# Folding the Fourier mixing of an attention and FNet kernel over features and over four classes of tokens

## The chip, the cores and the metric

The kernel runs on one core of a Trainium2 chip. A core has five engines that work side by side, each through its own instructions in order: TensorE (PE, matrix products, with its weight loads as a second row, PEld), VectorE (DVE), ScalarE (ACT), GpSimd (POOL) and SyncE (SP), which here only issues DMAs. They wait for each other by semaphores. The metric is device time in microseconds (us) of one launch.

## The reference

Two kinds of layer take turns, twice each, on `x` of 2048 tokens by 512 features, all in fp32: softmax attention with 32 heads of 16, and a Fourier mixing that keeps the real part.

```python
def _A_ref(x, wqkv, wo):
    B, S, D = x.shape
    H = 32; Dh = D // H
    qkv = (lambda x, *d: x.transpose(*d))((x @ wqkv).reshape(B, S, 3, H, Dh), 2, 0, 3, 1, 4)
    q, k, v = qkv[0], qkv[1], qkv[2]
    scores = jnp.einsum("bhqd,bhkd->bhqk", q, k) * Dh ** -0.5
    o = jnp.einsum("bhqk,bhkd->bhqd", _softmax(scores, axis=-1), v)
    return (lambda x, *d: x.transpose(*d))(o, 0, 2, 1, 3).reshape(B, S, D) @ wo

def _B_ref(x, dft_seq_re, dft_seq_im, dft_hid_re, dft_hid_im):
    a = jnp.einsum("bsd,ed->bse", x, dft_hid_re)
    b = jnp.einsum("bsd,ed->bse", x, dft_hid_im)
    return jnp.einsum("ts,bse->bte", dft_seq_re, a) - jnp.einsum("ts,bse->bte", dft_seq_im, b)

x = x + _A_ref(_layernorm(x), A_wqkv, A_wo)
x = x + _B_ref(_layernorm(x), ...)
x = x + _A_ref(_layernorm(x), A_wqkv, A_wo)
x = x + _B_ref(_layernorm(x), ...)
```

The four DFT matrices (2048x2048 and 512x512, cosine and sine) are inputs, so the kernel may use their symmetries only if it tests them.

## The kernel before

**Precision.** Where fp32 accuracy is wanted, an operand is split into a high part rounded to the fast format fp32r and a low part, the rest (`split`, L93: ACT writes the high part, DVE or POOL subtracts for the low one), and `mm3` (L102) makes three products. Other fp32 products are not split.

**Projection** (`project`, L266): normalises `x`, transposes it on PE (L321), makes q, k and v, and sends q and k through DRAM. The weights are loaded (`load_w`) and split (`split_w`) by quarters; for layer 2 this is done during the first mixing, by `after.open()`, `after.prepare()` and `split_w` calls between its last products (L953 to L964), and early in projection 2.

**Attention** (`attend`, L587): 32 units `u` (a pair of heads, half of the tokens) of 16 steps `kt`, 512 steps in all. A step makes four score products (`scores`, L511) into two of three PSUM tiles called `sc`, ACT takes the exponential of both (L517, 128x1024 each), and two steps later PE multiplies by the values (`pv`, L532). When a unit is done, `gather` copies its sums (L542), `pack` rearranges them by eight small DMAs on SP, and `normalize` divides (L563 to L566). The loads of the next unit (`load_k`, `load_q`, `load_m`) are issued on POOL's queue. From unit 17 on the `wo` tiles of the first half of the tokens are made between steps, and `fold` runs on POOL at units 21 and 23.

**The symmetry test.** In attention 1 only, the class `Symmetry` streams the token DFT matrix `ct` through free buffers, 32 groups of four tiles, one group at every 7 steps. POOL subtracts entries that should mirror each other, DVE takes the largest absolute value (`amax`, L131). At step 244 `finish` (L178) makes the maximum over partitions: DVE's L190, PE's transpose L192 into an `sc` tile, and DVE's L193 and L194 into `sflag`. At the end of each mixing a branch on `sflag` runs `general`, which uses no symmetry.

**Mixing** (`mix_layer`, L717). Tokens `s`, `1024 - s`, `1024 + s` and `2048 - s` share rows of the DFT, so `fold` (L646) adds and subtracts their four normalised tiles, and four classes `k` of half-size products remain: even and odd tokens, real and imaginary. `accumulate` (L753) multiplies the folded tokens by the split DFT, 48 products of 128x512 for a class; `evacuate` splits the result into `Uh` and `Ul`; `hid` (L860) multiplies by the features' DFT, 24 products per output pair; ACT copies one half out (`osb`, L871), DVE and POOL add to two tiles of `x` (L874 to L880), `layernorm` follows if there is a next layer (L86 to L89; the last step of it, L79, is put off to the next call of `ln_flush`), and SP stores. Two tokens that fold on themselves are `edge` products (L790), whose operands are put on three partitions by small DMAs, and a Nyquist row made apart. All matrices are split anew in each mixing (`split_c`, `split_f`, `load_d`).

The order is written out by hand: two chunks of `accumulate` and the edges, then the last unit's normalisation and the eight `wo` tiles of the second half of the tokens with `fold` of groups 2 and 3 (L807 to L827), then the other products of the even tokens, four `hid`, all products of the odd tokens, four `hid`.

## Time and profile before

| | us |
|---|---|
| median of 3 runs | 2620.58 (2619.74 to 2621.46) |
| the profiled execution | 2620.9 |
| its span, first to last instruction | 2619.1 |
| PE busy | 2494.2 (95%) |
| ACT busy | 2043.3 (78%) |
| DVE busy | 1252.7 (48%) |
| POOL busy | 744.3 (28%) |

The span falls into six stages, cut where one kind of work ends in the timeline: projection 1, attention 1, mixing 1, projection 2, attention 2, mixing 2. A busy share over the whole span is a mean of stages that have different limits, so each stage is read from its own windows, and a wait from its place in the timeline. An engine's idle time is told by the instruction that ended it.

### The profile page before, as it was taken

Reading aid. Unit: us, or ns where it says so; the run is one execution under the profiler, and the core shown is the slowest. Engines: PE = TensorE matmul, PEld = TensorE weight load, DVE = VectorE, ACT = ScalarE, POOL = GpSimd, SP = SyncE. Lnnn points to the kernel's source line nnn. Section 1 sums busy time; section 2 is a strip of 40 time slices with the busy share of each in tenths; the row PEclk is TensorE's granted clock in tenths of the full one; section 3 lists DMA queues with packets and bytes.
Section 4 is the critical chain, followed back from the end, with each engine's and each line's share of the span. In section 5 each row is a group of like instructions: output and inputs, shape, how many; then the busy total and the mean of one; then the engine's idle time right before and its main releaser. Section 6 shows DMA issues by size and latency. Waiting matters only on the chain. (4 is left out here: it accounts for less than half of the span.)

```text
span 2619.1 us, 37733 instructions
## 1 busy us (share of the span) xinstructions
PE 2494.2 (95%) x14853; PEld 1098.1 (42%) x14853; DVE 1252.7 (48%) x1555; ACT 2043.3 (78%) x2324; POOL 744.3 (28%) x1091
## 2 busy tenths in 40 slices
PE   7999999997999999986979999999999999999778
PEld 6753333332343333345767533333333433333456
...
GB/s 189 140 155 126 148 149 118 130 107 28 73 74 53 59 54 46 45 51 119 112 132 141 98 62 56 56 47 45 51 60 67 68 65 49 46 46 46 69 117 114
DMA packets 117132, 223.34 MB, mean 85 GB/s; under 512 B 29860, under 2 KB 38324, under 8 KB 110772
## 3 DMA queue, kind: packets, MB, share of 16 engines
...
## 5 line engine op out<-in xcount | busy, mean ns | idle before, releaser
L517 ACT ACTIVATE P<-sc 128x1024 f32<-128x1024 f32 x2048 | 1880.5, 1191 | 89.7 <-PE sc L511 89.7
L532 PE MATMUL po<-P,V 128*17 128x512 f32 x8192 | 1079.3, 599 | 0.4 <-ACT P L517 0.4
L511 PE MATMUL sc<-qs,ks 64*128 64x512 f32 x4096 | 939.4, 445 | 9.1 <-DMA ks<-kd 5.0
L511 PEld LDWEIGHTS sc<-qs,ks 64*128 64x128 f32 x4096 | 484.5, 184 | 876.0 <-ACT P L517 829.1
L563 DVE RECIPROCAL lpk<-lpk 32x512 f32<-32x512 f32 x128 | 427.6, 3340 | 198.4 <-DMA lpk<-oa 196.0
L542 DVE COPY oa<-po 17x512 f32<-17x512 f32 x256 | 175.9, 687 | 656.8 <-PE po L532 650.7
L257 POOL DMA_DIRECT2D ks<-kd x128 | 65.7, 513 | 968.8 <-PE sc L511 946.1
L532 PEld LDWEIGHTS po<-P,V 128*17 128x17 f32 x8192 | 136.3, 95 | 376.4 <-issue 355.0
L98 ACT ACTIVATE qh<-sc 128x512 fp32r<-128x512 f32 x64 | 38.2, 596 | 130.8 <-PE sc L105 125.9
L164 POOL TENSOR_TENSOR xh<-xh,xh 128x512 f32<-128x512 f32 x96 | 121.1, 1290 | 0.7
L89 POOL TENSOR_TENSOR rs<-ve,mhalf 128x1 f32<-128x1 f32 x64 | 44.9, 702 | 251.2 <-DVE ve L88 251.0
L365 POOL TENSOR_TENSOR sq<-qh 128x512 fp32r<-128x512 f32 x64 | 66.8, 1044 | 160.5 <-ACT qh L98 159.3
L104 PE MATMUL sc<-xTl,wh 128*128 128x512 f32 x256 | 101.2, 395 | 0.5 <-DVE xTl L96 0.4
L105 PE MATMUL sc<-xTh,wl 128*128 128x512 f32 x256 | 101.5, 397 | 0.0
L103 PE MATMUL sc<-xTh,wh 128*128 128x512 f32 x256 | 101.5, 396 | 0.0
L131 DVE TENSOR_REDUCE sym<-xh 128x1 f32<-128x512 f32 (+1 forms) x128 | 76.2, 615 | 51.4 <-POOL xh L164 47.6
L566 DVE TENSOR_TENSOR oT<-opk,oT 32x512 fp32r<-32x512 f32 x128 | 89.7, 700 | 4.4
L95 ACT ACTIVATE fh<-xh 128x512 fp32r<-128x512 f32 x32 | 18.9, 623 | 93.0 <-DVE xh L654 91.2
L564 DVE TENSOR_TENSOR opk<-opk,lpk 32x512 f32<-32x512 f32 x128 | 88.6, 692 | 4.5
L99 DVE SCALAR_TENSOR_TENSOR ql<-sc,qh 128x512 fp32r<-128x512 f32 x64 | 43.9, 687 | 94.7 <-ACT qh L98 93.7
L263 POOL DMA_DIRECT2D qs<-md x128 | 67.1, 525 | 29.3 <-DMA ks<-kd 29.3
L250 POOL DMA_DIRECT2D qs<-qd x128 | 64.7, 506 | 5.2 <-issue 5.2
...
## 6 DMA issues: line engine op xcount, KB each, us to landing
ks<-kd POOLq DMA_DIRECT2D x128, 256.0 KB, 5.0
xh<-ct SPq DMA_DIRECT2D x128, 256.0 KB
qs<-qd POOLq DMA_DIRECT2D x128, 128.0 KB, 5.4
ks<-kd POOLq DMA_DIRECT2D x128, 128.0 KB, 4.2
...
```

Source lines behind the costliest of these rows:

```text
L103: nc.tensor.matmul(ps, ah, bh, start=start, stop=False)
L104: nc.tensor.matmul(ps, ah, bl, start=False, stop=False)
L105: nc.tensor.matmul(ps, al, bh, start=False, stop=stop)
L131: nc.vector.reduce_max(self.m[:n, self.col:self.col + 1], d, axis=AX.X, apply_absolute_value=True)
L164: nc.gpsimd.tensor_tensor(T[g], T[g], T[0], op=op)
L511: nc.tensor.matmul(pss[hd][:, qb * 512:qb * 512 + 512], k[r:r + 64, kt * 128:kt * 128 + 128], q[r:r + 64, qb * 512:qb * 512 + 512], start= ...
L517: e = nc.scalar.activation(pt, pss[hd], AF.Exp)
L532: nc.tensor.matmul(o[32 * j:32 * j + DH + 1, :], self.V[:, kt, 2 * p + hd, :], P[hd][:, qb * 512:qb * 512 + 512], start=kt == 0, stop=kt = ...
L542: nc.vector.tensor_copy(oa[32 * j:32 * j + DH + 1, :], o[32 * j:32 * j + DH + 1, :])
L563: nc.vector.reciprocal(lpk[rr, c], lpk[rr, c])
L564: nc.vector.tensor_tensor(opk[rr, c], opk[rr, c], lpk[rr, c], op=ALU.mult)
L566: nc.vector.tensor_tensor(ot[rr, 1, c], opk[rr, c], ot[rr, 0, c].bitcast(F32), op=ALU.subtract)
```

## The change

Features are put into the order 0, 256, 1 to 255, 511 to 257 outside the kernel, and `fold` now also folds feature `j` with `512 - j`: 16 operations of 255 or 257 columns for 8 of 512, and classes of half the width again. Tokens 0 to 255 stand for four outputs each (`t`, `1024 - t`, `1024 + t`, `2048 - t`), so a layer has eight `hid` of 13 products with 256 or 258 columns, and the sums and differences of an even and an odd result (`combine`, `finish`) give the four tiles. Single tokens are rank-one fp32 products (`crow`, `drow`) and four `corners`. `Symmetry` also tests the features' DFT (36 groups, one at every 6.5 steps), and its POOL work writes the split DFT matrices to DRAM (`keep_c`, `halves`), from where mixing loads them. The split weights of projection 1 are written to DRAM (`save_w`) and loaded again (`open_w`). Folded groups 0 and 1 are split by POOL during attention (`split_g`, units 24 and 25; `fold` at units 21 and 22). The mixing begins with the even tokens' products over groups 0 and 1, which are all the data that they need.

```diff
 class Symmetry:
+        self.groups += [("d", part, c) for part in range(2) for c in range(2)]
+        self.m = pool_.tile([128, 200], F32, name="sym")
...
+    def halves(self, src, fixes=()):
+        n, w = src.shape
+        h = self.pool.tile([128, 258], F32R, name="symh", bufs=2)
+        l = self.pool.tile([128, 258], F32R, name="syml")
+        nc.gpsimd.tensor_copy(h[:n, :w], src)
...
+        nc.gpsimd.tensor_tensor(l[:n, :w], src, h[:n, :w].bitcast(F32), op=ALU.subtract)
...
+    def keep_c(self, T, part, i, j):
...
+        for hl, t in enumerate(self.halves(T[0][:, :w], fixes)):
+            c0 = 128 * (j % 2)
+            t = t.bitcast(F32)
+            nc.sync.dma_start(cs[k, half, hl, :, i % 2, c0:c0 + 128], t[:, 0:128])
...
     def mirror(self, d, t, part, i, j):
+        g.tensor_tensor(d[:, 256:384], t[:, 128:256], t[:, 0:128], op=op2)
...
+    def reduce(self):
+        self.mx = self.pool.tile([128, 1], F32, name="symmx")
+        nc.vector.reduce_max(self.mx, self.m, axis=AX.X)
+
     def finish(self):
         ps = sc_tile()
-        nc.tensor.transpose(ps[:1, :128], mx, ident)
+        nc.tensor.transpose(ps[:1, :128], self.mx, ident)
+        lim = self.pool.tile([1, 1], F32, name="symlim")
         nc.vector.reduce_max(sflag, ps[:1, :128], axis=AX.X)
-        nc.vector.tensor_tensor(sflag, sflag, self.scale, op=ALU.is_le)
+        nc.vector.tensor_tensor(lim, self.scale[:, 0:1], self.scale[:, 1:2], op=ALU.min)
+        nc.vector.tensor_scalar(lim, lim, TOL, None, op0=ALU.mult)
+        nc.vector.tensor_tensor(sflag, sflag, lim, op=ALU.is_le)
...
     def attend(self):
-                if i < 8 and i % 4 == 0 or i >= 8 and i % 7 == 1:
-                    sym.load(i // 4 if i < 8 else 1 + i // 7)
-                if i % 7 == 6:
-                    sym.compare(i // 7)
+                for n in range(len(sym.groups)):
+                    if i == max(0, 13 * n // 2 - 12):
+                        sym.load(n)
+                    if i == 13 * n // 2 + 6:
+                        sym.compare(n)
+                if i == 10:
+                    sym.finish_special()
                 if i == 244:
+                    sym.reduce()
+                if i == 262:
                     sym.finish()
...
+            if u == 0 and kt == 1 and self.first:
+                self.save_w()
...
 def fold(i, p_, tag, engine):
+    m = [t1[:, 0:255], t1[:, 255:510], t2[:, 0:255], t2[:, 255:510]]
+    for x, d in zip(X, m):
+        tt(d, x[:, 2:NR], x[:, NR:], ALU.subtract)
+        tt(x[:, 2:NR], x[:, 2:NR], x[:, NR:], ALU.add)
...
 def mix_layer(at, x_src, x_dst, after):
+    def product(out, k, half, ch, c):
+        f = features(k, ch)
+        ch_, cl_ = C[k, half]
+        for i in (2 * half, 2 * half + 1):
+            gh, gl = G[k // 2, i]
+            for n, (g, w) in enumerate(((gh, ch_), (gh, cl_), (gl, ch_))):
+                nc.tensor.matmul(out, g[:, f], w[:, i % 2, c], ...)
+        if (k, half) == (0, 0):
+            nc.tensor.matmul(out, z[0:1, f], crow[0:1, c], start=False, stop=True)
+
+    def seq(half):
+        t1, t2, t3 = sc_tile(), sc_tile(), sc_tile()
...
+    load_c(0, 0)
+    at.pack(2 * NP - 1, *at.last, engine=nc.scalar)
...
+    for k, out, row in seq(0):
+        evacuate(k, out, row, 0)
...
     for t in range(8, 12):
         at.wo_mm(t, wps[t - 8], range(ND - 1))
     for qb in range(2):
         at.normalize(2 * NP - 1, qb, *at.last)
     for t in range(8, NT):
...
         if t == 12:
             ln_flush()
             fold(2, bl, "tf", nc.vector)
+            split_g(2, nc.scalar, nc.gpsimd)
     ln_flush()
     fold(3, bl, "tf", nc.vector)
+    split_g(3, nc.scalar, nc.gpsimd)
     at.ab.release()
+    if after is not None:
+        after.open_w()
...
+    def hid(cls, q):
+        ps = sc_tile()
+        re, im = ps[:, 0:258], ps[:, 512:768]
...
+        nc.scalar.activation(ims[:, 2:NR], im[:, 0:255], AF.Copy)
+        return re, ims
+
+    def combine(engine, re, ims, name, bufs):
+        zt = br.tile([128, 767], F32, name=name, bufs=bufs)
+        engine.tensor_tensor(zt[:, 0:NR], re[:, 0:NR], ims, op=ALU.subtract)
+        engine.tensor_tensor(zt[:, NR:512], re[:, 2:NR], ims[:, 2:NR], op=ALU.add)
+        engine.tensor_tensor(zt[:, 512:767], re[:, 2:NR], ims[:, 2:NR], op=ALU.subtract)
+        return zt
...
+            re, ims = hid(cls, q)
+            res = br.tile([128, 258], F32, name="res", bufs=2)
+            nc.scalar.activation(res, re, AF.Copy)
+            zp[cls, q] = combine(nc.gpsimd, res, ims, "zp", 4)
+    for k, out, row in seq(1):
+        evacuate(k, out, row, 1)
...
+    def finish(cls, q):
+        re, ims = hid(cls, q)
+        zq = combine(nc.vector, re, ims, "zq", 2)
+        zt = zp[cls, q]
+        zs = br.tile([128, 767], F32, name="zs", bufs=1)
+        nc.gpsimd.tensor_tensor(zs, zt, zq, op=ALU.add)
+        nc.vector.tensor_tensor(zt, zt, zq, op=ALU.subtract)
+        t = 4 * (2 * cls + q)
+        add_plain(nc.vector, xq[t], zs, ALU.add)
+        add_swapped(nc.gpsimd, xq[t + 1], zt, ALU.add)
+        add_plain(nc.vector, xq[t + 2], zt, ALU.add)
+        add_swapped(nc.gpsimd, xq[t + 3], zs, ALU.add)
...
+    finish(0, 1)
+    corners()
+    finish(0, 0)
+    finish(1, 0)
+    finish(1, 1)
     ln_flush()
     with tc.If(gv == 0):
         general(x_src, x_dst, after)
+    if after is not None:
+        after.open()
+        after.prepare()
```

Three places in the programs' order follow. The first is DVE at the end of the symmetry test in attention 1 (`sym` the maxima by group, `oa`, `lpk`, `opk` and `oT` one unit's sums, divisors and result). Before, the reduction over groups stands behind the normalisation of unit 14:

```order
L542 COPY oa<-po 17x512 x4
L563 RECIPROCAL lpk<-lpk 32x512
L564 TENSOR_TENSOR opk<-opk,lpk 32x512
L565 CAST oT<-opk 32x512
L566 TENSOR_TENSOR oT<-opk,oT 32x512
L563 RECIPROCAL lpk<-lpk 32x512
L564 TENSOR_TENSOR opk<-opk,lpk 32x512
L565 CAST oT<-opk 32x512
L566 TENSOR_TENSOR oT<-opk,oT 32x512
L131 TENSOR_REDUCE sym<-symrows 64x1 x5
L190 TENSOR_REDUCE symmx<-sym 128x1
L193 TENSOR_REDUCE sflag<-sc 1x1
```

The same engine and place with the change:

```order
L284 TENSOR_REDUCE symmx<-sym 128x1
L654 COPY oa<-po 17x512 x4
L675 RECIPROCAL lpk<-lpk 32x512
L676 TENSOR_TENSOR opk<-opk,lpk 32x512
L677 CAST oT<-opk 32x512
L678 TENSOR_TENSOR oT<-opk,oT 32x512
L675 RECIPROCAL lpk<-lpk 32x512
L676 TENSOR_TENSOR opk<-opk,lpk 32x512
L677 CAST oT<-opk 32x512
L678 TENSOR_TENSOR oT<-opk,oT 32x512
L290 TENSOR_REDUCE sflag<-sc 1x1
```

The maximum (`symmx`) has moved ahead of a unit's normalisation, now that of unit 15, and the reading of PE's transpose (L290) stands behind it.

The second place is PE behind the last product of attention (`ch`, `cl` the split DFT, `fh`, `fl` a folded group's two parts, before):

```order
L758 MATMUL sc<-ch,fh_13914 128x512 x4
L758 MATMUL sc<-cl,fh_13914 128x512 x4
L758 MATMUL sc<-ch,fl_13915 128x512 x4
L758 MATMUL sc<-ch,fh_13922 128x512 x4
L758 MATMUL sc<-cl,fh_13922 128x512 x4
L758 MATMUL sc<-ch,fl_13923 128x512 x4
L790 MATMUL sc<-c_13883,z_13882 128x512 x4
L103 MATMUL po<-woh,oT 128x512
L104 MATMUL po<-wol,oT 128x512
```

With the change, the same engine and place (the folded groups' parts are `xh` tiles; these rows are one of the fourteen such runs of six):

```order
L888 MATMUL sc<-ch_14275,xh_12568 128x258
L888 MATMUL sc<-cl_14276,xh_12568 128x258
L888 MATMUL sc<-ch_14275,xh_12569 128x258
L888 MATMUL sc<-ch_14275,xh_12803 128x258
L888 MATMUL sc<-cl_14276,xh_12803 128x258
L888 MATMUL sc<-ch_14275,xh_12804 128x258
L891 MATMUL sc<-crow,xh_10892 128x258
```

The products have half the columns, and the edge products from three partitions (L790) have become one fp32 product of one partition (L891), ahead of the `wo` products as before.

The third place is DVE at the first output tiles of a mixing with a normalisation behind it. Before:

```order
L874 TENSOR_TENSOR xb<-po,xb 128x512
L878 TENSOR_TENSOR xb<-po,xb 128x512
L86 BN_STATS st<-xb 128x6
L87 BN_AGGR mv<-st 128x2
L88 TENSOR_SCALAR ve<-mv 128x1
L86 BN_STATS st<-xb 128x6
L87 BN_AGGR mv<-st 128x2
L88 TENSOR_SCALAR ve<-mv 128x1
L79 TENSOR_SCALAR xh_14498<-xb,mv,rs 128x512
```

With the change (`zq` an odd result, `zp` the even one and then the difference, `zs` the sum, `x_...` the residual tiles):

```order
L1012 TENSOR_TENSOR zq<-sc,iqs_14724 128x257
L1013 TENSOR_TENSOR zq<-sc,iqs_14724 128x255
L1014 TENSOR_TENSOR zq<-sc,iqs_14724 128x255
L1066 TENSOR_TENSOR zp<-zp,zq 128x767
L1018 TENSOR_TENSOR x_14716<-x_14716,zs 128x512
L1018 TENSOR_TENSOR x_14720<-x_14720,zp 128x512
L93 BN_STATS st<-x_14716 128x6
L94 BN_AGGR mv<-st 128x2
L95 TENSOR_SCALAR ve<-mv 128x1
```

Two tiles per `hid` have become four, and the combination of two results stands ahead of the adds.

More of the change, by code (lines that the diff above doesn't have):

```diff
@@ L28 @@
 NQ = 4
+NR = 257
 @with_exitstack
@@ L543, in gather, with pack @@
             return oa, opk, lpk
-        def pack(self, u, oa, opk, lpk):
+        def pack(self, u, oa, opk, lpk, engine=nc.sync):
             r0 = 32 * (u % NP % 4)
@@ new lines, in mix_layer, with evacuate @@
+        Uh, Ul = {}, {}
+        def evacuate(k, out, row, half):
+            n = 258 if (k, half) == (0, 0) else 256
+            Uh[k] = bl.tile([128, 2, 258], F32R, name=f"uh{k}")
+            Ul[k] = bl.tile([128, 2, 258], F32R, name=f"ul{k}")
+            split(Uh[k][:, :, 0:n], Ul[k][:, :, 0:n], out[:, :, 0:n])
+            if row is not None:
+                lr[k] = bl.tile([1, 258], F32, name=f"lr{k}", bufs=2)
+                nc.scalar.activation(lr[k][:, 0:256], row, AF.Copy)
+        cp = bl.tile([128, 2, 2], F32, name="cp")
@@ L1030 @@
     y = np.empty((S, D), np.float32)
-    y[order] = r.results[0]["out"]
+    y[np.ix_(order, fo)] = r.results[0]["out"]
     return y.reshape(1, S, D)
```

569 lines of the change are left out of this document (291 added, 278 removed).

## The prediction

> **What bounds the kernel now.** I read the page first, then the windows by stage, the timelines of the stages that the change touches, and the waits and group rows inside them. The windows give start and end, length, busy time of PE, weight load, DVE, ACT and POOL with counts, granted clock, DMA share and GB/s; in order: projection 1, attention 1, mix 1, projection 2, attention 2, mix 2.
> ```profile
> 0.00:158.00 158.00, 141.92 (x625) 110.43 (x625) 77.36 (x140) 44.77 (x70) 60.79 (x73) 1.00 0.51 166
> 158.00:1148.60 990.60, 975.86 (x6289) 337.10 (x6289) 512.18 (x595) 940.90 (x1025) 341.11 (x528) 0.99 0.42 87
> 1148.60:1327.20 178.60, 131.34 (x517) 100.86 (x513) 108.46 (x199) 41.54 (x76) 71.29 (x68) 0.86 0.38 120
> 1327.20:1482.00 154.80, 148.63 (x648) 116.88 (x649) 47.79 (x70) 41.73 (x64) 43.42 (x52) 0.96 0.43 130
> 1482.00:2449.40 967.40, 967.05 (x6267) 333.04 (x6267) 427.16 (x424) 937.41 (x1022) 178.33 (x328) 1.00 0.32 53
> 2449.40:2619.10 169.70, 129.36 (x513) 99.74 (x513) 79.70 (x128) 36.96 (x68) 49.37 (x42) 0.88 0.34 109
> L517 ACT ACTIVATE P<-sc 128x1024 f32<-128x1024 f32 x2048 | 1880.5, 1191 | 89.7 <-PE sc L511 89.7
> ```
> Both attentions run at the pace of ACT's exponentials: 940.9 of 990.6 us, and by the page's group row 1880.5/2048 = 0.92 each, two a step: a step of 1.83 us, 29.3 a unit of 16. That pace stays. The mixes hold 348.3 us, and PE is busy in 260.7 of them: there the change can gain.
>
> **Attention 1: the end of the symmetry test.** Timeline around it (start, duration, engine, line; in brackets the idle time before and who ended it):
> ```profile
> 614.06 2.84 DVE L542 COPY oa<-po 17x512 f32<-17x512 f32 x4 [10.73 <-PE po L532]
> 619.26 3.34 DVE L563 RECIPROCAL lpk<-lpk 32x512 f32<-32x512 f32 x1 [2.35 <-DMA lpk<-oa]
> 628.96 0.68 DVE L566 TENSOR_TENSOR oT<-opk,oT 32x512 fp32r<-32x512 f32 x1
> 630.85 0.37 PE L192 MATMUL sc<-ident,symmx 128*1 128x128 f32 x1 [13.19 <-DVE symmx L190]
> 632.41 1.94 ACT L517 ACTIVATE P<-sc 128x1024 f32<-128x1024 f32 x2 [13.76 <-PE sc L511]
> 635.39 1.94 ACT L517 ACTIVATE P<-sc 128x1024 f32<-128x1024 f32 x2 [1.05 <-PE sc L511]
> 637.65 11.10 ACT L517 ACTIVATE P<-sc 128x1024 f32<-128x1024 f32 x12 [0.31 <-PE sc L511]
> ```
> PE's transpose waits 13.2 us for the maximum, which DVE makes only after unit 14's normalisation; ACT loses 13.76 + 1.05 + 0.31 = 15.1 us. The maximum now comes early, and the transpose stands at step 262, five steps behind unit 15's gather. It will not wait. But its PSUM tile is one of three `sc`, and what releases it is DVE's reduction into `sflag`, which DVE reaches behind the normalisation, about 16 us after the gather (614.06 to 629.6 today). Five steps of 1.83 us are 9.2 us, so scores stand still for some 6.7 us, plus 1 cold. **Net −7**, between −15.1 (no wait left) and 0 (the wait only moves).
>
> POOL, not on the path, gets more: 36 groups for 32, one at every 6.5 steps for 7, plus hi and lo halves of the DFT matrices, and DMA stores on SP that wait for them.
> ```profile
> 160.00:520.00 360.00, 359.25 (x2321) 124.28 (x2320) 219.87 (x287) 349.01 (x381) 190.88 (x277) 1.00 0.58 136
> POOL xh L139 <- DVE sym L131: 133.2, 13, 12.7
> 355.90 0.45 POOL L139 TENSOR_TENSOR xh<-xh 128x128 f32<-128x128 f32 x1
> ```
> Of 360 us POOL works 191 and waits 133 for DVE. Per unit of 29.3 us it works 15.5. A group gains three or four operations of the 128-column kind, 1.4 to 2 us, and with 2.46 groups a unit for 2.29 the work comes to 15.5 x 1.08 + 2.46 x 1.7 = 21. I price it at 0, hidden by those waits; without that cover it is rival B. `save_w` sends 6 MB at the start of attention 1, beside a DMA share of 0.58; also hidden.
>
> **Mix 1, up to the finish.** DVE timeline (the last unit's normalisation, residual adds of the `wo` tiles, last fold, first and last rows of the finish), and one row of the stage's waits:
> ```profile
> 1160.86 3.35 DVE L563 RECIPROCAL lpk<-lpk 32x512 f32<-32x512 f32 x1
> 1171.60 0.69 DVE L566 TENSOR_TENSOR oT<-opk,oT 32x512 fp32r<-32x512 f32 x1
> 1176.65 0.69 DVE L583 TENSOR_TENSOR xr<-po,xr 128x512 f32<-128x512 f32 x1 [4.36 <-PE po L105]
> 1180.62 0.69 DVE L583 TENSOR_TENSOR xr<-sc,xr 128x512 f32<-128x512 f32 x1
> 1182.82 0.68 DVE L583 TENSOR_TENSOR xr<-sc,xr 128x512 f32<-128x512 f32 x1
> 1208.50 2.75 DVE L654 TENSOR_TENSOR xh<-t,xh 128x512 f32<-128x512 f32 x4
> 1241.71 0.69 DVE L874 TENSOR_TENSOR xb<-po,xb 128x512 f32<-128x512 f32 x1 [4.29 <-PE po L105]
> 1323.95 1.48 DVE L79 TENSOR_SCALAR xh<-xb,mv,rs 128x512 f32<-128x512 f32 x1
> PE sc L790 <- DMA z<-zl: 8.7, 1, 8.7
> ```
> Before, the last unit's normalisation ends at 1172.3, but PE had stood 8.7 us for a small DMA (L790) and brings the first `wo` tile late. The edge operands that went through DRAM-to-row DMAs are gone; even tokens' products stand first with their operands split beforehand. DVE evacuates them ahead of the normalisation, which keeps its start near 1160.5 (48 products by 0.12, the 12 with one weight column, K=1 ones, half of it at a low clock, 10 us, then two evacuations). So the adds begin at 1172: eight tiles at the pitch 1182.82 − 1180.62 = 2.2 are 17.5, flushes 1.5, two folds 11. A fold is now 16 operations of 256 columns; four of 512 take 2.75, 0.69 each, so one of 256 lies between half, 0.34, and 0.69; I take 0.34, 5.5 a fold. Fold 3 ends at **1203** for 1211.25 (1208.50 + 2.75).
>
> Now 256-column products. Prices: a chain of 512-column ones, and transposes with 128 columns, with their weight loads:
> ```profile
> 2566.37 11.32 PE sc L758 x48
> 1332.90 0.86 PEld L321 LDWEIGHTS sc<-ident,xh 128*128 128x128 f32 x8 [0.68 <-DVE xTl L96]
> 1332.90 1.10 PE L321 MATMUL sc<-ident,xh 128*128 128x128 f32 x8 [0.28 <-DVE xTl L96]
> 1158.00:1172.00 14.00, 7.94 (x24) 6.01 (x25) 12.38 (x11) 3.33 (x7) 5.48 (x4) 0.63 0.35 113
> ```
> 11.32/48 = 0.236 is the upper bound, 8 loads in 0.86 = 0.108 the lower, since each product brings a load; I take 0.12. After 1203: the split of fold 3 to 1206 (ACT, then POOL by 1.29 twice); the four even-token `hid` results go through ACT copies and two buffers into POOL (2.2 each); the odd tokens' products (48 by 0.12, plus rows, 9 us) and the first `hid`. Of these about 15 stand one behind the other, and 3 come on top because PE starts cold (the clock fell to 0.63 where PE waited): the finish begins at **1221**, and with all products of the layer done but its own; before, the first add of the finish came at 1241.71 with half of the products still behind it.
>
> [...]
>
> **Mix 1, the finish.** Group rows of the stage:
> ```profile
> L86 DVE BATCH_NORM_STATS2 st<-xb 128x6 f32<-128x512 f32 x16 | 11.1, 691 | 10.9 <-POOL xb L879 10.6 <-POOL xb L880 0.3
> L89 POOL TENSOR_TENSOR rs<-ve,mhalf 128x1 f32<-128x1 f32 x24 | 16.7, 696 | 32.4 <-DVE ve L88 32.3
> L79 DVE TENSOR_SCALAR xh<-xb,mv,rs 128x512 f32<-128x512 f32 x16 | 9.6, 598 | 0.4 <-POOL rs L89 0.4
> L879 POOL TENSOR_TENSOR xb<-xb,osb 128x512 f32<-128x512 f32 x8 | 10.3, 1289 | 10.4 <-ACT nuh L95 5.1 <-DVE xb L874 3.2 <-issue 2.1
> 1327.27 5.35 PE L321 MATMUL sc<-ident,xh 128*128 128x128 f32 x24 [13.62 <-DVEq L969]
> ```
> Each of four `finish` calls gives DVE three combine operations (1.0), `zt` on 767 columns (0.9 at the same 1.3 ns a column), two adds (1.2), about 1 of waiting for POOL's `zs`, and four normalisations (0.69 and two short ones, 1.15, plus a flush at a 0.46 pitch: 6.4): **10.6**. POOL has 1.9 (767 columns at 1.29/512), two adds of 1.3 and small ones, four L89 of 0.7: 7.5, beneath. Four are 43; corners four small operations, 1.3; their rows' DMAs 2, like the 2.35 that DVE waited for small ones above; last flush 1: 1268. From DVE's last row to the next stage it is 1327.27 − 1325.43 = 1.8 now, so projection 2 begins at 1270: **mix 1 122 for 178.6, −57**.
>
> The weights of layer 2 come as 4 MB of halves ahead of 2 MB of `x` on SP, from about 1195. What DMA moved at its busiest, and in this mix:
> ```profile
> 0.00:50.00 50.00, 36.30 (x155) 27.08 (x156) 36.44 (x65) 17.66 (x27) 26.63 (x33) 1.00 0.68 233
> 1190.00:1200.00 10.00, 5.10 (x17) 3.85 (x16) 9.65 (x18) 2.30 (x4) 3.46 (x3) 0.82 0.44 146
> ```
> At 233 GB/s for a share of 0.68, the full rate is some 340 (an estimate from the first row): 6 MB take 18 to 26 us and land at 1213 to 1221, when the adds want `x`. Taken as 0; rival C. Projection 2 loses its splits, which run beside PE: 0.
>
> **Mix 2** has no normalisation in the finish. Its way to the finish is that of mix 1, 72.4 us (1221 − 1148.6). There POOL sets the pitch: 1.9 + 2.6 + hand-over = 4.9 each, three and a last of 5.9 = 20.6. Behind the last POOL row come the store and the end:
> ```profile
> 2612.21 1.26 POOL xb L880
> ```
> 2619.1 − 2613.5 = 5.6. Together 99 for 169.7: **−71**.
>
> **Sum.** −7 − 57 − 71 = −135 against the profiled execution, 2620.9 (span 2619.1 and 1.8 around it), which stands 0.3 above the median of three, 2620.58, nothing to correct. That is 2486. Each mix has some 20 hand-overs between engines on this path which I did not count, 0.1 each: +4. **2490.** With the two ends of the symmetry term, folds at 0.69 (+11 each mix at most, partly the same wait) and the products' lower bound, its own range is 2470 to 2512.
>
> **Rivals.**
> A, weight loads don't hide under products half as long: 256 columns cost 0.236. Then even tokens' products +5.5 and what follows fold 3 +6.4 in each mix: **2514**. For it: loads average 188 ns there, as in the row below. Against: the eight transposes above, half the size again, take 0.14 each with loads included. Chance 0.08. [...]
> ```profile
> L103 PEld LDWEIGHTS sc<-Dh,Uh 128*128 128x128 f32 x32 | 6.0, 188 | 1.2
> L532 PE MATMUL po<-P,V 128*17 128x512 f32 x8192 | 1079.3, 599 | 0.4 <-ACT P L517 0.4
> ```
> B, POOL becomes the bound in attention 1: 21 us of work plus waits for DVE exceed 29.3 by 2 us a unit. From then the `ks` and `qs` loads, issued on POOL's queue, come late, and PE waits at each unit's start: 15 units by 2, with today's slack the size of a wait (12.7 at most) not enough: +30, **2520**. For it the 133 us of waiting, which are a chain with DVE, not free time; against: 169 of 360 us idle. Chance 0.13.
> C, `x` and weights land late in mix 1: 6 MB at the 146 GB/s of the second row take 43 us, 17 past 1221; the tiles are used over the finish, so a part hides: +13, **2503**. Chance 0.06.
> D, the other side: the symmetry flag says no, since the stricter test now takes in features too, and the general path runs at each branch: 640 full fp32 products a layer, each two instructions (as the 4 products a step of L532 above are 8192 in 1024 steps), at 0.236 are over 300 us in each mix, **3200** or more. It decides at the largest mirrored difference over 2^-34 of the largest entry, 5.8e-11. The change is then undone wholly. The matrices worked out from the reference's formulas differ by far less (1.5e-12 for tokens, 4.1e-13 for features). Chance 0.01.
>
> **Chances.** Forecast 0.70, B 0.13, A 0.08, C 0.06, D 0.01; 0.01 for other slower ends, 0.01 for none. The range 2466 to 2530 holds the forecast's own range and the rivals A, B and C with some play. Faster by over 0.2% (5 us, about what a measurement of this kernel can tell from no change): 0.97; within 0.2%: 0.01; slower: 0.02.
>
> **What would show it.** In the new profile: the transpose of the test with no wait ahead and ACT idle some 7 us near it; a mix 1 of 122 and a mix 2 of 99 us; 256-column products 0.12 apart; `finish` calls 10.6 and 4.9 apart, bounded by DVE and POOL; unit starts in attention 1 without PE waiting for `ks`. It is wrong if the mixes are bound by another engine or a DMA, or if attention 1 grows.

## The result and the profile after

The changed kernel takes **2551.17 us** (median of 4 runs, 2546.70 to 2551.46) beside 2621.02 (4 runs, 2619.74 to 2623.40) for the kernel before: a ratio of 0.9728 [0.9712, 0.9745] (in brackets a 95% interval). It is faster, by 70 us where 131 were forecast, and the time lies above the range of 2466 to 2530. The profiled execution took 2551.33, its span 2549.5.

The windows of the changed kernel by stage, cut at the same marks as before except one (start and end, length, busy time of PE, weight load, DVE, ACT and POOL, granted clock, DMA share, GB/s):
```profile
0.00:157.40 157.40, 140.36 (x625) 110.90 (x626) 77.52 (x141) 44.87 (x70) 61.47 (x75) 1.00 0.51 166
157.40:1178.30 1020.90, 984.15 (x6289) 337.52 (x6290) 523.51 (x611) 941.81 (x1024) 406.88 (x698) 0.98 0.47 98
1178.30:1314.50 136.20, 69.83 (x360) 54.76 (x357) 86.89 (x197) 12.67 (x30) 52.59 (x63) 0.75 0.40 141
1314.50:1457.00 142.50, 137.80 (x626) 111.01 (x626) 46.13 (x68) 36.47 (x56) 43.30 (x48) 0.99 0.45 146
1457.00:2431.70 974.70, 973.86 (x6289) 337.51 (x6289) 427.75 (x424) 940.07 (x1024) 194.35 (x364) 1.00 0.32 54
2431.70:2549.50 117.80, 69.32 (x360) 54.57 (x356) 64.06 (x133) 12.67 (x30) 40.48 (x46) 0.79 0.38 127
```
Against the rows of before (the cut between projection 2 and attention 2 lay elsewhere there, so these two are taken together):

| stage | before | forecast | after | miss |
|---|---|---|---|---|
| projection 1 | 158.0 | 158.0 | 157.4 | −0.6 |
| attention 1 | 990.6 | 983.6 | 1020.9 | **+37.3** |
| mix 1 | 178.6 | 122 | 136.2 | **+14.2** |
| projection 2 and attention 2 | 1122.2 | 1122.2 | 1117.2 | −5.0 |
| mix 2 | 169.7 | 99 | 117.8 | **+18.8** |

With the 4 us that the forecast added for hand-overs, the misses come to 61: the distance from 2490 to 2551. PE's busy time in the two mixes fell from 260.7 to 139.2 us, as the folding promises, but their length fell by only 94: PE is now busy for about half of them, at a granted clock of 0.75 and 0.79. And attention 1 grew by 30 us although ACT's busy time there is what it was, 941.8 for 940.9.

ACT's timeline in that stage (start, duration, engine, line; in brackets the idle time before and who ended it):
```profile
445.05 1.94 ACT L629 ACTIVATE P<-sc 128x1024 f32<-128x1024 f32 x2 [3.93 <-PE sc L623]
...
474.22 1.94 ACT L629 ACTIVATE P<-sc 128x1024 f32<-128x1024 f32 x2 [4.21 <-PE sc L623]
...
607.84 1.94 ACT L629 ACTIVATE P<-sc 128x1024 f32<-128x1024 f32 x2 [13.69 <-PE sc L623]
611.22 27.61 ACT L629 ACTIVATE P<-sc 128x1024 f32<-128x1024 f32 x30 [1.44 <-PE sc L623]
651.66 1.94 ACT L629 ACTIVATE P<-sc 128x1024 f32<-128x1024 f32 x2 [12.83 <-PE sc L623]
...
694.45 1.94 ACT L629 ACTIVATE P<-sc 128x1024 f32<-128x1024 f32 x2 [0.59 <-PE sc L623]
696.98 1.94 ACT L629 ACTIVATE P<-sc 128x1024 f32<-128x1024 f32 x2 [0.59 <-PE sc L623]
699.51 1.94 ACT L629 ACTIVATE P<-sc 128x1024 f32<-128x1024 f32 x2 [0.60 <-PE sc L623]
702.17 18.48 ACT L629 ACTIVATE P<-sc 128x1024 f32<-128x1024 f32 x20 [0.72 <-PE sc L623]
```
The end of the symmetry test (the last four rows) costs 2.5 us, less than forecast. New are four stalls at unit starts, two of them of 13 us. Around the first of these, on PE, POOL, SP and DVE:
```profile
587.42 0.45 POOL L166 TENSOR_TENSOR syml<-xh,symh 128x128 fp32r<-128x128 f32 x1 [8.75 <-DMA cs<-syml]
588.28 10.72 SPq L144 DMA_DIRECT2D xh<-dt  x4
592.79 0.55 POOL L369 DMA_DIRECT2D ks<-kd  x1
599.10 12.56 SPq L663 DMA_DIRECT2D lpk<-oa  x1
606.03 0.76 PE L623 MATMUL sc<-qs,ks 64*128 64x512 f32 x1 [12.86 <-DMA qs<-md]
620.90 3.34 DVE L675 RECIPROCAL lpk<-lpk 32x512 f32<-32x512 f32 x1 [24.61 <-DMA lpk<-oa]
631.93 0.73 POOL L232 TENSOR_TENSOR xh<-xh 128x255 f32<-128x255 f32 x1 [27.89 <-DVE sym L153]
```
And what DMA moved there, in 40 slices of 1 us from 575 to 615, with two of its issues (KB each, median us to landing):
```profile
GB/s 25 86 27 25 88 41 326 262 25 25 27 23 25 70 51 250 236 20 27 268 164 225 131 180 193 33 25 31 27 25 27 25 27 25 27 25 27 57 74 76
...
ks<-kd POOLq DMA_DIRECT2D x2, 256.0 KB, 8.8
xh<-dt SPq DMA_DIRECT2D x2, 254.0 KB
```
Over the last third, for 12 us on end, only 25 to 33 GB/s move. Two loads of the feature matrix `dt` are of 127 rows, 254 KB: at 25 GB/s 10 us each. What stands behind them comes late: a store of the test's `syml`, for which POOL waits 8.75 us before it can issue the next `ks` loads; those loads themselves (PE stands 12.86); the sums `lpk`, for which DVE waits 24.6; and then POOL, which waits 27.9 for DVE, so that the next unit's loads are late as well. From 600 to 612 us the DMA share is 0.09 at 27 GB/s, and one of the core's 16 DMA engines, busy alone, would be 0.06. That it is the number of rows that makes these transfers slow is so far a guess, which two of the runs below test; how it would do so isn't shown.

In mix 1, the rows that mark its steps, on ACT, PE and DVE:
```profile
1185.19 0.60 ACT L102 ACTIVATE uh<-sc 128x516 fp32r<-128x516 f32 x1 [7.92 <-DMA opk<-oa]
1188.10 0.46 PE L888 MATMUL sc<-ch,xh 128*128 128x256 f32 x1 [3.36 <-DVE cpi L950]
1195.58 3.35 DVE L675 RECIPROCAL lpk<-lpk 32x512 f32<-32x512 f32 x1
1206.03 0.69 DVE L696 TENSOR_TENSOR x<-po,x 128x512 f32<-128x512 f32 x1
1210.71 0.80 PE L110 MATMUL sc<-woh,oT 128*128 128x512 f32 x1 [6.31 <-DVE x L696]
1228.63 0.79 PE L110 MATMUL sc<-woh,oT 128*128 128x512 f32 x1 [6.48 <-DVE x L696]
1240.58 2.48 DVE L780 TENSOR_TENSOR xh<-xh,xh 128x257 f32<-128x257 f32 x6
1263.25 0.43 DVE L1012 TENSOR_TENSOR zq<-sc,iqs 128x257 f32<-128x257 f32 x1 [1.24 <-ACT iqs L1007]
```
Set against the forecast, from the start of the stage (1148.6 then, 1178.3 now):

| mix 1 | forecast | after | of it new in this step |
|---|---|---|---|
| last unit's normalisation starts | 11.9 | 17.3 | +5.4 |
| residual adds start | 23.4 | 27.7 | −1.1 |
| last fold ends | 54.4 | 64.8 | +6.1 |
| first `zq` of the finish | 72.4 | 85.0 | +2.2 |
| stage ends | 122 | 136.2 | +1.6 |

### The profile page after: what moved, and what is told of

Read it like the earlier page. It is cut to its first block, busy times and chain, and to the rows that moved or that the text cites. A ratio compares the mean times of both kernels' runs of the same rounds, so it can differ in the third digit from the quotient of the medians.

```text
span 2549.5 us, 37261 instructions
## 1 busy us (share of the span) xinstructions
PE 2375.3 (93%) x14539; PEld 1006.3 (39%) x14539; DVE 1225.9 (48%) x1573; ACT 1988.6 (78%) x2234; POOL 799.1 (31%) x1292
## 5 line engine op out<-in xcount | busy, mean ns | idle before, releaser
L644 PEld LDWEIGHTS po<-P,V 128*17 128x17 f32 x8192 | 136.4, 95 | 379.9 <-issue 357.5
L153 DVE TENSOR_REDUCE sym<-xh 128x1 f32<-128x512 f32 (+6 forms) x142 | 87.6, 630 | 82.5 <-POOL xh L222 59.2
L436 PE MATMUL sc<-ident,xh 128*128 128x128 f32 x128 | 19.5, 311 | 54.3 <-DVEq L1090 43.0
```

Source lines behind the costliest of these rows:

```text
L153: nc.vector.reduce_max(self.m[:n, self.col:self.col + 1], d, axis=AX.X, apply_absolute_value=True)
L644: nc.tensor.matmul(o[32 * j:32 * j + DH + 1, :], self.V[:, kt, 2 * p + hd, :], P[hd][:, qb * 512:qb * 512 + 512], start=kt == 0, stop=kt = ...
```

## The experiments

All are edits of the changed kernel, but for one of the kernel before. Times are medians, of four runs where nothing else is said; the stage columns are lengths in each profiled execution (from the first scores to the start of the last gather copies, from there to the next stage or the end), which differ by a few tenths from the windows above. How much a stage varies by itself is seen where the edit doesn't touch it: attention 1 takes 1016.8 to 1021.0 (the changed kernel stands at the upper end), mix 1 134.4 to 137.7, mix 2 117.7 to 118.2. Differences of that size show nothing.

| kernel | us (range) | ratio to before | att. 1 | mix 1 | mix 2 |
|---|---|---|---|---|---|
| before | 2621.02 (2619.74–2623.40) | 1 | 990.1 | 178.6 | 169.8 |
| after | 2551.17 (2546.70–2551.46) | 0.9728 [0.9712, 0.9745] | 1021.0 | 136.1 | 117.7 |
| b1_127_in_before | 2616.04 (one run, 2622.30 beside it) | – | 988.9 | 174.6 | 172.5 |
| e1_rows112 | 2523.60 (2519.88–2530.42) | 0.9625 [0.9608, 0.9643] | 995.6 | 137.7 | 118.2 |
| e5_pace7_alone | 2542.50 (2536.72–2546.28) | 0.9707 [0.9691, 0.9724] | 1011.2 | 134.4 | 117.7 |
| e4_rows112_pace7 | 2508.90 (2507.86–2510.94) | 0.9569 [0.9553, 0.9585] | 978.4 | 135.8 | 117.9 |
| e2_two_syml | 2543.17 (2540.97–2544.16) | 0.9702 [0.9686, 0.9718] | 1016.6 | 136.4 | 117.8 |
| m1_pack_on_pool | 2540.03 (2533.92–2542.64) | 0.9686 [0.9664, 0.9707] | 1019.3 | 132.2 | 114.9 |
| w1_psum_of_wo | 2537.41 (2535.23–2540.38) | 0.9681 [0.9665, 0.9697] | 1018.5 | 129.8 | 114.0 |
| g1_even_hid_early | 2550.10 (2545.76–2553.65) | 0.9736 [0.9720, 0.9752] | 1017.2 | 135.5 | 119.8 |
| f1_own_difference | 2549.61 (2547.79–2550.66) | 0.9728 [0.9712, 0.9744] | 1019.5 | 137.5 | 120.7 |
| p1_finish_in_two_parts | 2546.79 (2544.48–2550.61) | 0.9724 [0.9708, 0.9740] | 1016.8 | 134.4 | 116.6 |
| f3_finish_on_dve | 2546.70 (2545.03–2550.17) | 0.9716 [0.9700, 0.9732] | 1019.4 | 135.5 | 115.2 |
| x1_finish_all_dve | 2544.72 (2544.18–2547.90) | 0.9710 [0.9694, 0.9727] | 1018.8 | 134.7 | 115.0 |
| c1_all | 2487.86 (2486.57–2491.66) | 0.9493 [0.9477, 0.9508] | 979.2 | 129.5 | 107.2 |
| c2_without_early_hid | **2484.31** (2483.99–2486.91) | 0.9479 [0.9464, 0.9495] | 975.4 | 126.3 | 107.4 |

### Attention 1: transfers of 127 rows, or too many groups?

**Rows of 112 and 15.** Each 127-row transfer of the test becomes two; no other split was run.
```diff
-                    nc.sync.dma_start(t[:k, :], dt[part, r:r + k, :])
+                    for a, b in ((0, 128),) if k == 128 else ((0, 112), (112, 127)):
+                        nc.sync.dma_start(t[a:b, :], dt[part, r + a:r + b, :])
...
-                        nc.sync.dma_start(ds[1, hl, 1:128, 1, 0:256], t[:127, 0:256].bitcast(F32))
+                        for a, b in ((0, 112), (112, 127)):
+                            nc.sync.dma_start(ds[1, hl, 1 + a:1 + b, 1, 0:256], t[a:b, 0:256].bitcast(F32))
```


> Of the changed kernel, only the DMAs of 127 rows (two loads of the feature matrix in each of two groups of the symmetry test, two stores of its halves) are made as 112 and 15 rows. Theory 1: a DMA of 127 rows drains at about 25 GB/s, some 10 us for 254 KB; two in a row hold SP's queue, the packing DMAs of a unit queue behind them, DVE waits for those, POOL waits for DVE, and POOL's loads of the next unit come late. Then both stalls of PE in attention 1 of 13.7 and 12.8 us go, attention 1 falls from 1021 to 992 to 996 us, and the time to 2520 to 2526. Theory 2: POOL has too much work in attention 1 whatever the DMAs do: one stall at least stays above 8 us, and the time is above 2538.

The 13 us stalls are gone; attention 1 is 25.4 us shorter, the kernel 27.6. ACT's timeline there, and one issue of the DMA view from 570 to 600:
```profile
475.53 1.94 ACT L631 ACTIVATE P<-sc 128x1024 f32<-128x1024 f32 x2 [5.72 <-PE sc L625]
...
598.57 1.94 ACT L631 ACTIVATE P<-sc 128x1024 f32<-128x1024 f32 x2 [3.39 <-PE sc L625]
```
```profile
ks<-kd POOLq DMA_DIRECT2D x2, 256.0 KB, 4.8
```
The `ks` loads land in 4.8 us for 8.8. Smaller stalls remain, so this is not the whole.

**The same slow transfer in the kernel before.** Two tiles of another matrix, `ct`, are loaded as 127 rows and one.
```diff
-                    nc.sync.dma_start(t, ct[part, j, 4 * i + g])
+                    for a, b in ((0, 127), (127, 128)) if n == 20 and g < 2 else ((0, 128),):
+                        nc.sync.dma_start(t[a:b, :], ct[part, j, 4 * i + g, a:b, :])
```


> The kernel before, with two tiles of one group of its symmetry test (group 20, about 415 us) loaded by a DMA of 127 rows and one of a single row each, in place of 128 rows. Theory 1: by the row count alone each 127-row DMA moves 254 KB at some 25 GB/s, so DMA shows 20 us in a row at 25 to 30 GB/s and one sixteenth of its share, where the 256 KB loads of 128 rows beside it take 2 to 3 us; the next packing DMAs on SP queue behind it. This kernel has slack there, so its time stays at 2615 to 2632. Rival: the slowness comes of the place or alignment in the feature matrix, or of the writes beside it, and here the 127 rows move at over 100 GB/s.

DMA from 405 to 445 in 40 slices (its share in tenths and what it moved), and SP's row for the loads:
```profile
DMA  8998999910000000100000259999999969811421
GB/s 213 197 197 131 201 182 148 119 23 14 27 20 25 27 25 35 41 27 25 27 25 27 37 205 379 330 334 248 299 164 191 164 109 230 115 18 41 51 72 31
```
```profile
413.25 17.76 SPq L127 DMA_DIRECT2D xh<-ct  x10
```
The rate is again mostly 25 to 27 GB/s, for some 15 us where 20 were expected; from 414 to 421 the DMA share is below 0.1 in every slice. So it is the 127 rows, not the matrix or the place. But the kernel lost nothing by it (attention 1 988.9 for 990.1, in its one run): at that place of the slower plan there was slack to take it up.

**The pace.** Groups one every 7 steps, as before, in place of 6.5.
```diff
-                        if i == max(0, 13 * n // 2 - 12):
+                        if i == max(0, 7 * n - 13):
...
-                        if i == 13 * n // 2 + 6:
+                        if i == 7 * n + 6:
...
-                    if i == 244:
+                    if i == 256:
...
-                    if i == 262:
+                    if i == 276:
```


> Of the changed kernel, only the pace of the symmetry test is put back to one group in every 7 steps (its end at steps 256 and 276); the DMAs of 127 rows stay. Theory 1: two 127-row transfers in a row still hold SP's queue for 20 us in two groups, so at least one stall of over 8 us remains, attention 1 is 995 to 1010 us and the time 2525 to 2540. Rival, theory 2 alone: the dense pace made all of it, attention 1 falls to 978 to 984 as with both edits, and the time to 2509 to 2515.

Alone, it shortens attention 1 by 9.8 us, to 1011.2 (theory 1 said 995 to 1010): the stalls of 4 us are gone, the two large ones stay.
```profile
625.30 1.94 ACT L629 ACTIVATE P<-sc 128x1024 f32<-128x1024 f32 x2 [16.60 <-PE sc L623]
...
670.30 1.94 ACT L629 ACTIVATE P<-sc 128x1024 f32<-128x1024 f32 x2 [13.29 <-PE sc L623]
```
**Both edits together:**

> Of the changed kernel, the DMAs of 127 rows as 112 and 15, and the symmetry test at one group in every 7 steps again, its end at steps 256 and 276 for 244 and 262. Theory 2 for what is left in attention 1 (stalls of 3.6, 5.7 with 1.4, 3.4 with 1.4 us at unit starts): POOL's work per unit is too dense; at 7 steps these stalls fall to 5 us in all, attention 1 to 983 to 988 for 995.6, the time to 2511 to 2517. Rival: the stalls come of waits for DVE and DMA whatever the pace, and the time stays within 3 us of 2524.

Attention 1 falls by 42.6 us, to 978.4: below the kernel before by 11.7, and below the range expected, with ACT running 493 us without a stall.
```profile
183.87 493.28 ACT L631 ACTIVATE P<-sc 128x1024 f32<-128x1024 f32 x538 [2.66 <-PE sc L625]
```
The two edits give 25.4 and 9.8 alone and 42.6 together. So two causes are shown, the slow transfers the larger, the density the smaller, and they share some 7 us that only both take away (up to 12, if the changed kernel's attention 1 is taken at 1016.8). What of the denser plan it is, POOL's work, DVE's maxima or the transfers, all of which the slower pace thins out together, isn't shown.

**A second buffer for `syml`**, for which POOL waited 8.75 us.
```diff
-            l = self.pool.tile([128, 258], F32R, name="syml")
+            l = self.pool.tile([128, 258], F32R, name="syml", bufs=2)
```
(A tile of zeros was halved, and written in two DMAs, to make room.)

> Of the changed kernel, only the low halves of the symmetry test get a second buffer (the zero row becomes shorter, written in two DMAs). Theory 3: POOL's waits for the stores of low halves (20.3 us in attention 1, 8.75 ahead of the first stall) make the loads late; then attention 1 falls by 10 us or more, to 2541 or less in all. Theory 1: the stores themselves stand behind the 127-row transfers and the packing stays late, so the two stalls stay within 3 us of 13.7 and 12.8 and the time is 2546 to 2552.

The first large stall falls from 13.7 to 5.0, the second grows from 12.8 to 16.5. Attention 1 is 4.4 shorter, but two runs that don't touch it come to 1016.8 and 1017.2 as well, so no gain is shown, and neither theory's forecast came true. POOL's wait carries the delay only at one of the two places; with the slow transfer still there it comes through by another way.

### The mixes up to the finish

**The last unit's small DMAs off ACT's queue.** ACT issues the transfers of `pack`, about 0.6 each, ahead of the first evacuation of the even tokens' products.
```diff
-        at.pack(2 * NP - 1, *at.last, engine=nc.scalar)
+        at.pack(2 * NP - 1, *at.last, engine=nc.gpsimd)
```


> Of the changed kernel, only the eight packing DMAs of the last unit are issued on POOL's queue, not on ACT's. Theory: ACT's queue is held 6 us by these issues ahead of the first evacuation, PE waits for PSUM (3.4 us) and runs the rest cold, so the last normalisation begins 17 us after the last product of attention; then it begins after 12, each mixing is 4 to 6 us shorter and the time 2539 to 2544. Rival: the evacuations are paced by PE's products and not by ACT's start, or the packed rows come later from POOL's queue: the start moves by less than 1.5 us and the time stays at 2548 to 2552.

The evacuation no longer waits for them:
```profile
1181.32 0.60 ACT L102 ACTIVATE uh<-sc 128x516 fp32r<-128x516 f32 x1 [5.89 <-PE sc L891]
```
The normalisation starts 13.75 us after the last gather copies begin, in both mixes, for 17.1 and 16.8 (12 were expected), and the kernel gains 11 us. In mix 1, 3.9 of them are in the stage, in mix 2 2.8; the rest lies in differences of 1 to 2 us in stages that the edit doesn't touch, and is no gain of it.

**Own PSUM tiles for the `wo` products.** In the changed kernel two output tiles share one tile of PSUM, and PE twice waits, 6.31 and 6.48 us in mix 1, for DVE's add to one half of it before it writes again.
```diff
-        w3 = sc_tile()
-        wps = [po_tile(), po_tile(), w3[:, :512], w3[:, 512:]]
-        for t in range(8, 12):
+        wps = [po_tile(), po_tile()] + [sc_tile()[:, :512] for _ in range(3)]
+        for t in range(8, 13):
...
-            ps = wps[t - 8] if t < 12 else po_tile() if t < 14 else w3[:, (t - 14) * 512:(t - 13) * 512]
+            ps = wps[t - 8] if t < 13 else po_tile() if t < 15 else sc_tile()[:, :512]
```


> Of the changed kernel, the eight wo tiles of the second half of the tokens use the three free PSUM tiles sc one by one, not two halves of one, and five of them are begun ahead of the normalisation for four. Theory: PE waits twice 6.4 us in each mixing for DVE's add of the other half of the same tile, falls to half clock and brings tiles 12 and 15 late (DVE waits 2.0 and 2.9 us); from the first add to the end of the last fold it is then 32 us for 37, and the time 2539 to 2544. Rival: DVE's own work sets that stretch, and it stays above 35 us and the time at 2548 to 2552.

From the first residual add to the end of the last fold 31.6 us, for 37.0: the forecast's 31. PE's waits in mix 1 (line, for whom, total, times, longest):
```profile
PE sc L110 <- DVE x L696: 8.6, 1, 8.6
PE sc L110 <- ACT res L1026: 6.5, 1, 6.5
```
PE still waits once, but with its products for tile 12 already made, and DVE doesn't wait for it. The kernel gains 13.8 us, 6.3 and 3.7 of them in the mixes as cut.

**Even tokens' `hid` results earlier**, behind `wo` tile 12, while DVE still adds and folds.
```diff
             if t == 12:
+                zp = {}
+                for cls in range(2):
+                    for q in range(2):
+                        re, ims = hid(cls, q)
+                        res = bl.tile([128, 258], F32, name="res", bufs=2)
+                        nc.scalar.activation(res, re, AF.Copy)
+                        zp[cls, q] = combine(nc.gpsimd, res, ims, "zp", 4)
                 ln_flush()
```


> Of the changed kernel, the four products of the even tokens with the features' matrix, their copies by ACT and their combination by POOL stand behind wo tile 12, beside the second fold, not behind the last one. Theory: 20.2 us pass from the end of the last fold to the first odd result on DVE, of which ACT's copies, POOL's 8.3 us and the two buffers between them take some 7 on the path; then it is 12 to 15 us, and the time 2536 to 2542. Rival: the products then stand ahead of wo tiles 13 to 15, the folds end later by as much, and the time stays at 2547 to 2552.

Nothing gained: the last fold ends 68.3 and 70.5 us after the last gather copy (64.6 and 64.0 without), and the finish begins at 84.1 and 86.5 (84.8 and 84.2). What was moved out of the way to the finish delays the folds by as much or more, as the rival said.

### The finish

**A tile of its own for the difference**, which overwrites `zt` and so had to wait for POOL's sum of it.
```diff
-            nc.vector.tensor_tensor(zt, zt, zq, op=ALU.subtract)
+            zd = br.tile([128, 767], F32, name="zd")
+            nc.vector.tensor_tensor(zd, zt, zq, op=ALU.subtract)
```
(The two adds that use the difference read `zd`.)

> Of the changed kernel, only the difference of even and odd results goes to a buffer of its own, not over the even result, so that DVE need not wait for POOL's sum to have read it. Theory: in each of the eight finish calls a round trip POOL, DVE, POOL (1.9 us of DVE waiting for the sum, 1.1 us of POOL waiting for the difference) sets the pitch; then mixing 2's pitch falls from 6.6 to 5.5 us, mixing 1's from 12.9 to about 11.5, and the time to 2538 to 2543. Rival: DVE's larger operations slow POOL's when they run at the same time (POOL's addition of 510 columns takes 1.70 us there and 1.25 alone), so the pitch stays within 0.5 us and the time at 2547 to 2552.

No difference, as the rival said. The wait ahead of the difference goes, but DVE's operations now run beside POOL's, and both get slower: in mix 2's first call POOL's sum takes 2.59 us for 1.83 and DVE's second add 1.76 for 0.69.

**The calls in two parts**, so that the next call's sum on POOL runs beside DVE's part of this one.
```diff
-        finish(0, 1)
+        a, b = start(0, 1), start(0, 0)
+        finish(*a)
         corners()
-        finish(0, 0)
-        finish(1, 0)
-        finish(1, 1)
+        a = start(1, 0)
+        finish(*b)
+        b = start(1, 1)
+        finish(*a)
+        finish(*b)
```


> Of the changed kernel, each finish is cut in two, and the next one's products, combination and POOL's sum are issued ahead of the present one's adds and normalisations (a second buffer for the sum). Theory: DVE's wait for the sum (1.9 us in each of eight) is hidden, mixing 1's pitch falls from 12.9 to 10.8 to 11.5, the time to 2542 to 2547. Rival: DVE and POOL slow each other as in the run with its own difference buffer (additions 1.75 for 0.69 us), the pitch stays above 12.2 and the time at 2548 to 2552.

The result can't be told from the changed kernel's, and in mix 1 the calls still come 12.6 and 12.9 apart, as the rival said. Its rows show why; the same operations, alone (the first row and the last) and beside the other engine:
```profile
1259.42 1.84 POOL L1065 TENSOR_TENSOR zs<-zp,zq 128x767 f32<-128x767 f32 x1 [9.73 <-DVE zq L1014]
...
1261.46 0.95 DVE L1069 TENSOR_TENSOR zp<-zp,zq 128x767 f32<-128x767 f32 x1
1261.62 2.48 POOL L1065 TENSOR_TENSOR zs<-zp,zq 128x767 f32<-128x767 f32 x1 [0.36 <-DVE zq L1014]
1262.32 2.32 DVE L1018 TENSOR_TENSOR x<-x,zs 128x512 f32<-128x512 f32 x1
...
1264.57 0.68 DVE L1018 TENSOR_TENSOR x<-x,zp 128x512 f32<-128x512 f32 x1
```
DVE's add takes 2.32 us where it takes 0.68: it starts 0.70 behind POOL's sum and ends 0.54 behind its end, as if it ran only when POOL was done. And POOL's sum, which starts 0.16 behind DVE's difference, takes 0.64 longer than alone. What makes the two engines slower side by side isn't shown.

**POOL's part of the finish on DVE**, in mix 2 alone, then in both mixes.
```diff
-            nc.gpsimd.tensor_tensor(zs, zt, zq, op=ALU.add)
+            fe = nc.gpsimd if after is not None else nc.vector
+            fe.tensor_tensor(zs, zt, zq, op=ALU.add)
...
-            add_swapped(nc.gpsimd, xq[t + 1], zt, ALU.add)
+            add_swapped(fe, xq[t + 1], zt, ALU.add)
...
-            add_swapped(nc.gpsimd, xq[t + 3], zs, ALU.add)
+            add_swapped(fe, xq[t + 3], zs, ALU.add)
```


> Of the changed kernel, in the last mixing (which has no normalisation behind it) all of the finish is put on DVE, nothing on POOL. Theory: DVE takes 0.6 us for an addition for which POOL takes 1.3 to 1.7, and the round trips go; a finish is then 3 x 0.33 + 2 x 0.88 + 4 x 0.6 and two small ones, some 5.5 us for 6.6, the last 5.5 for 9.1, and the time 2543 to 2547. Rival: without POOL beside it DVE becomes the bound at 6.5 us or more, and the time stays at 2548 to 2552.

For both mixes `fe = nc.vector`:

> Of the changed kernel, the sum and the two swapped additions of each finish are put on DVE in both mixings; POOL keeps only the small powers of the normalisation. If DVE and POOL take turns on large operations (an addition of DVE takes 2.3 us for 0.7 and POOL's sum 3.7 for 1.8 where they run at the same time), nothing is lost by giving POOL's to DVE: a finish is then DVE's own 11.3 us for 12.9 in mixing 1 (1.0 combining, 1.75 sum and difference, 2.7 additions, 5.9 normalisation) and 5.5 for 6.6 in mixing 2, and the time 2539 to 2546. Rival: POOL's work did run beside DVE's; DVE then takes over 3.7 us more a finish in mixing 1, the pitch grows above 13.5 us there, and the time is 2551 to 2558.

One engine alone is no slower than the two. Mix 2 is 2.5 and 2.7 us shorter: where POOL's sums came 6.6 apart, DVE's come 5.5 to 5.6 apart (6.9 with the corners between), and the last call with the store takes 12.2 for 15.1. In mix 1 the three pitches of the second kernel add up to 35.1 for 37.8; the stage as cut, 1.4 shorter, is within its own variation. DVE's rows of one call there:
```profile
1261.07 0.96 DVE L1066 TENSOR_TENSOR zs<-zp,zq 128x767 f32<-128x767 f32 x1
1262.06 0.96 DVE L1067 TENSOR_TENSOR zp<-zp,zq 128x767 f32<-128x767 f32 x1
```
The sum that takes POOL 1.8 takes DVE 0.96, with no hand-over. Against the changed kernel the ratios' intervals overlap; the runs' ranges (2544.18 to 2547.90, and 2546.70 to 2551.46) nearly part.

### Together

First all that promised something: rows, pace (with the end of the test at step 284), `pack`, PSUM tiles, the finish in two parts with DVE alone in mix 2, and the early `hid`:

> The changed kernel with all of the edits together: DMAs of 112 and 15 rows, one group in 7 steps and the test's end at step 284, packing on POOL's queue, PSUM tiles one by one for wo, even products early, the finish in two parts, and in the last mixing on DVE alone. If the effects are of different stretches and add, 43 us from attention 1 and its end 2, 7 from the packing, 10 from wo's PSUM, 3 from the last finish and what the two other runs of this set give (5 to 20) make 2460 to 2482. If the mixing's stretches share one limit (DVE), the mixing's edits give half of that, and the time is 2483 to 2496.

Then without the early `hid` and the two parts, and DVE alone in both finishes:

> As the kernel with all edits, but the even products at their old place and the finish in one part, all of it on DVE in both mixings. If the early products cost the folds what they save (the folds end 4 to 6 us later with them), and DVE alone needs 11.3 us a finish, this is faster than the kernel with all edits: 2473 to 2484. Rival: the early products do help once PSUM of the wo tiles is free, and this is slower, 2488 to 2496.

The first, at 2487.86, lies in the range for stretches that share a limit. The second has the best median, 2484.31, just above its own range, 0.9479 [0.9464, 0.9495] of the time before and 66.9 below the changed kernel; the two intervals overlap, so that it beats the first is likely but not shown. 45.6 of its 66.9 lie in attention 1, 9.8 and 10.3 in the mixes. Its folds end 55.8 us after the last gather copy in both mixes, for the 54.4 of the forecast. That this kernel comes near the forecast's 2490 is partly luck: attention 1 ends 8.2 below the 983.6 forecast, the mixes 4.3 and 8.4 above theirs.

## Why the prediction was wrong

**The step that failed** is the cost of the test's extra work in attention 1: "I price it at 0, hidden by those waits; without that cover it is rival B". The symmetry term beside it stood at −7; with 2.5 us left of 15.1 it was −12.6, four steps 0.6 late each instead of a halt (the transpose holds one of three `sc` tiles, and PE went on in the other two). So the extra work cost 30.3 + 12.6 = 43 us instead of 0. The runs split it: transfers of 127 rows at 25 to 27 GB/s (25.4 alone), the denser plan (9.8 alone), 42.6 with both taken away. That leaves the symmetry term: 978.4 is 11.7 below the kernel before. The prediction counted POOL's operations and the bytes, and neither was the larger trouble: POOL works 406.9 of 1020.9 us, and from 160 to 520 us 17.7 a unit, for the 21 of the prediction. It looked at no transfer's shape, though the change's code names the 127 rows.

**Rival B** (0.13, 2520) had the kind of the loss right, late `ks` and `qs` loads on POOL's queue and PE waiting at unit starts, but its trigger, POOL's work and waits over 29.3 us a unit, can hold for the smaller part at most, and even there it isn't shown: in `e1_rows112`, too, POOL waits for DVE's maxima, 132.3 us in 13 waits from 158 to 720, the longest 12.7, and how much of the smaller stalls comes of these waits was not taken apart.

**Mix 1 and 2 up to the finish**: three terms were too small. (1) The start of the normalisation, "which keeps its start near 1160.5", came 5.4 us later: the ACT queue's small DMAs held the first evacuation, PE stood 3.36 us and went on at a granted clock of 0.53. Moving them gave 3.1 to 3.4 of it. (2) Adds and folds were priced by DVE alone, 31 us; PE's waits for PSUM halves, for which DVE then waits 2.04 and 2.94 us, made them 37. Tiles of their own gave 31.6. (3) From the last fold to the finish it took 20.2 for 18. PE is busy for 16.4 of these, and from 1244.9 to 1253.0, at a granted clock of 0.50, its products stand 0.215 us apart instead of 0.119, some 3.6 us more (an estimate from these spacings), about the 3 that the prediction added for a cold start; the rest wasn't taken apart.

**The finish**: in mix 1 the sum was nearly right (51.2 for 49.6). The pitches of 13.0, 12.9 and 11.8 hold the corners' operations (1.3, in the first) and the waits for their rows (1.9, in the second), both as priced; a call without them takes 11.1 to 11.8 for 10.6, since DVE waits 1.9 to 2.0 us for POOL's sum, not "about 1". In mix 2 the sum was 33.5 for 26.6. POOL sets the pitch there, as forecast, but its sums come 6.6 apart for 4.9; the rows of the last call:
```profile
2536.98 1.80 POOL L1065 TENSOR_TENSOR zs<-zp,zq 128x767 f32<-128x767 f32 x1
2539.84 0.57 POOL L1021 TENSOR_TENSOR x<-x,zp 128x2 f32<-128x2 f32 x1 [1.07 <-DVE zp L1066]
2540.39 1.69 POOL L1022 TENSOR_TENSOR x<-x,zp 128x510 f32<-128x510 f32 x1
```
The operations on two columns, some 0.7 a call, weren't counted; POOL waits 1.07 us for DVE's difference, where 0.4 stood for the hand-over; and the first addition takes 1.69 beside DVE's adds, where the second takes 1.25. The last call with the store took 15.1 for 11.5.

**Right**: the 256-column products stand 0.12 apart at a granted clock of 1.00 (1183.0 to 1184.7), as PE's first two rows here, so rival A fell; `x` and the weights came in time, since DVE waits only for the corner rows, as in DVE's row, so rival C fell; and the flag held, so D did.
```profile
1184.34 0.28 PE L888 MATMUL sc<-cl,xh 128*128 128x256 f32 x1
1184.46 0.28 PE L888 MATMUL sc<-ch,xh 128*128 128x256 f32 x1
...
1188.35 0.42 PE L888 MATMUL sc<-cl,xh 128*128 128x256 f32 x1
1188.56 0.63 PE L888 MATMUL sc<-ch,xh 128*128 128x256 f32 x2
```
```profile
1282.94 0.69 DVE L93 BATCH_NORM_STATS2 st<-x 128x6 f32<-128x512 f32 x1 [1.51 <-DMA x<-x]
```
But behind PE's waits of 3.36 and 4.83 us they stand 0.21 apart, as in PE's last two rows (granted clock 0.53 from 1188.1 to 1191.5, and 0.50 from 1244.9 to 1253.0): in mix 1 that is so for 48 of 228 products of 256 or 258 columns, and costs PE some 4.6 us (an estimate from the spacings of 0.215 and 0.119), not all of it on the path. In the finish it is not so: the 48 of its four `hid` run from 1260.5 to 1270.9 at a granted clock of 1.00, nearly all 0.12 apart.

Projections and attention 2, priced at 0, gained 5.6 us; why wasn't tried.

**The range** took in B, A and C one at a time, but not a loss in attention 1 together with terms of the mixes that were all summed at their least, each engine running without the others' waits.

**What stays open**: the 7 us or more that only both edits of attention 1 take away, what of the denser plan costs time, the 20 us between the last fold and the finish (20.2 and 21.0 still in the best kernel), and how much of the mixes is the clock (0.75 and 0.80 still in the best kernel), which no run set apart from PE's waits.
